# Batches 0 and 1 of an attention and MLP kernel: heads transposed straight from their load by column tiles, and one Ln, Exp and normalise for two units

## The chip, the cores and the metric

The kernel runs on one core of one Trainium2 chip. A core has TensorE (PE in the profile; matmuls and transposes, results in the PSUM banks), VectorE (DVE), ScalarE (ACT), GpSimd (POOL; here it only issues transfers) and SyncE (SP; likewise). The metric is the time on the device for one execution, in microseconds: the median of several runs. Before the change it is 430.69 us (three runs, 430.52 to 430.87).

## What is computed

Attention over 8 batches, 12 heads, 448 positions and 64 features a head, with one added to the denominator of the softmax; then a two-layer MLP with a squared ReLU on the 3584 tokens.

```python
def _attn_ref(q, k, v):
    scale = 1.0 / np.sqrt(q.shape[-1])
    scores = scale * np.matmul(q, k.transpose(0, 1, 3, 2))
    m = np.max(scores, axis=-1, keepdims=True)
    e = np.exp(scores - m)
    attn = e / (np.sum(e, axis=-1, keepdims=True) + np.exp(-m) + 1e-09)
    return np.matmul(attn, v).astype(np.float32)

def _moe_ref(x, w_in, w_out):          # x: 3584 x 768, from all heads; d_ff = 2048
    h = x @ w_in
    r = np.maximum(h, 0.0)
    g = r * r
    return (g @ w_out).astype(np.float32)
```

## The kernel before

The instructions of each engine stand in the order in which the program names them; a pool's buffer is given out again when its last reader is done. Work goes by units: a unit is a pair of heads and a stretch of queries. Batch 0 is cut in two stretches of 192 and 256 queries, so that units 0 to 5 are its pairs with 192 queries, units 6 to 11 the same pairs with 256; units 12 to 17 are batch 1, with all 448 queries, and so on. `RUN` is 4 and `P` is 112: a head's 448 positions lie as 112 partitions of 4 each. `NPAIR` is 6, `D` 64, `S` 448.

Batches 2 to 7 are transposed by the DMA. Batches 0 and 1 come in their natural order, are regrouped on VectorE so that the two heads of a pair lie side by side, and are transposed on TensorE, 128 columns (two heads) at a time:

```python
    def regroup(b, pr):
        for name in "qk":
            f = flat.tile([P, RUN, 2, D], FP16, name=f"flat{name}")
            nc.vector.tensor_copy(f, naturals[name, b, pr].rearrange("p h t d -> p t h d"))
            flats[name, b, pr] = f

    def transposes(b, pr):
        tp = m_psum.tile([128, 2, 512], FP16, name="mp")
        for i, name in enumerate("qk"):
            for s in range(RUN):
                nc.tensor.transpose(tp[:, i, P * s:P * s + P], flats[name, b, pr][:, s], ident[0:P, 0:P])
        if b not in qks:
            qks[b] = qk_pool.tile([128, 3, COLS], FP16, name="qk")
        nc.vector.tensor_copy(qks[b][:, 0:2, pr * S:(pr + 1) * S], tp[:, :, 0:S])
```

The scores of a unit are matmuls into one of two score buffers (`s_psum`, two banks each), and ScalarE's exponential (L155) empties them into `et`. VectorE adds the four chunks of `et` into `es` (L200 to L208). Then:

```python
    def values(u, et, xp, c):
        b, pr, _, n = u
        for kk in (2 * c, 2 * c + 1):
            for h in range(2):
                nc.tensor.matmul(xp[64 * h:64 * h + 64, 0:n], vns[b][:, 2 * pr + h, kk, :],
                                 of_head(chunk(et, u, c, kk), u, h), start=(kk == 0), stop=(kk == RUN - 1))

    def row_sums(u, es):
        n = u[3]
        total = es[:, 0:2 * S] if n == S else es[:, 4 * S - 2 * n:4 * S].rearrange("p (h n) -> p h n", h=2)
        zp = m_psum.tile([128, 512], FP32, name="mp")
        for h in range(2):
            nc.tensor.matmul(zp[64 * h:64 * h + 64, 0:n], ones, of_head(total, u, h), start=True, stop=True)
        rcp = z_pool.tile([128, S], FP32, name="rcp")
        nc.scalar.activation(out=rcp[:, 0:n], in_=zp[:, 0:n], func=AF.Ln, bias=one_b)
        nc.scalar.activation(out=rcp[:, 0:n], in_=rcp[:, 0:n], func=AF.Exp, scale=-1.0)
        return rcp

    def normalise(u, xp, rcp):
        b, pr, q0, n = u
        if b // 2 not in xts:
            xts[b // 2] = xt_pool.tile([128, DCH, 2 * S], FP16, name="xt")
        c = b % 2 * S + q0
        nc.vector.tensor_mul(xts[b // 2][:, pr, c:c + n], xp[:, 0:n], rcp[:, 0:n])
```

The MLP runs between the pieces of the units, a share at a time, so that TensorE has other work while it waits. For its first block (128 tokens) a ReLU in two of four groups goes to ScalarE:

```python
            else:
                nc.vector.tensor_scalar(out=rt[:, 0:m], in0=hp[:, 0:m], scalar1=0.0, scalar2=None, op0=ALU.max)
            g = g_pool.tile([128, 512], FP16, name=f"g{f0}")
            nc.vector.tensor_mul(g[:, 0:m], rt[:, 0:m], rt[:, 0:m])
```

The loop over units, and the warming matmuls ahead of it, which multiply zeros. (b, p) is pair p of batch b; (0, p) is transposed in unit p - 1, (1, p) in unit 8 + p. GpSimd issues the loads in this order: values and q, k of batch 0; half of `w_in`; q, k of (1,0) to (1,2); the rest of `w_in`; q, k of (1,3) to (1,5); half of batch 1's values; `w_out`:

```python
# ... (tables of when each pair is regrouped and transposed, keep_warm, take_up)
    keep_warm(3)
    regroup(0, 1)
    et = es = None
    share = [0.0]

    def take_up(i):
# ...
    for i in range(NU + 1):
        u = units[i] if i < NU else None
        prev = units[i - 1] if i > 0 else None
        xp = rcp = None
        if prev:
            pet, pes = et, es
            xp = x_psum.tile([128, 512], FP32, name="xp")
        if u:
            b, pr = u[0:2]
            if pr == 0 and 0 < b and b + 1 < B:
                load_v(b + 1, 0, NPAIR)
                stage(b + 1)
            et = e_pool.tile([P, RUN * 2 * S], FP16, name="et")
            es = e_pool.tile([P, 4 * S], FP16, name="es")
            scores(u, et, 0)
            if i == 0:
                keep_warm(4)
            elif i < NPAIR:
                keep_warm(1)
                scores(u, et, 1)
            if i == NPAIR:
                rcp = row_sums(prev, pes)
                values(prev, pet, xp, 0)
                values(prev, pet, xp, 1)
                normalise(prev, xp, rcp)
                take_up(i - 1)
            if i in transpose_at:
                transposes(*transpose_at[i])
            if i in regroup_at and i < NPAIR:
                regroup(*regroup_at[i])
            drain(share[0] * (0.45 if i != NPAIR else 0.0))
            if i == 0 or i >= NPAIR:
                scores(u, et, 1)
        if prev and i != NPAIR:
            rcp = row_sums(prev, pes)
            values(prev, pet, xp, 0)
            values(prev, pet, xp, 1)
            if i < NPAIR:
                keep_warm(1)
        if i in regroup_at and i >= NPAIR:
            regroup(*regroup_at[i])
        halved[0] = u is not None
        drain(share[0] * 0.15)
        for step in range(3):
            if u:
                add_chunks(u, et, es, step)
            drain(share[0] * (0.15, 0.1, 0.15)[step])
        halved[0] = False
        if prev and i != NPAIR:
            normalise(prev, xp, rcp)
            take_up(i - 1)
        if u and b and pr == 2 and b + 1 < B:
            transposed_loads(b + 1)
    drain(1e12)


# ---- launch: one core; inputs and outputs as the reference has them ----
_INS = ['q', 'k', 'v', 'moe_w_in', 'moe_w_out']
_OUTS = [((3584, 768), 'float32')]


def kernel(**inputs):
    import numpy as _np
    import concourse.bacc as _bacc
    import concourse.tile as _tile
    from concourse import mybir as _mybir
    from concourse.bass_utils import run_bass_kernel_spmd as _run

    nc = _bacc.Bacc("TRN2", target_bir_lowering=False, num_devices=1)
    arrays, args = {}, []
    for name in _INS:
        a = _np.ascontiguousarray(inputs[name])
        if a.dtype.kind in "iu":
```

`queue` takes up MLP parts once their tokens are done: after unit 5 the first layer for tokens 0 to 127, after unit 11 the first layer for tokens 128 to 383 and the second for 0 to 383. `drain(x)` puts in MLP matmuls worth about x ns; with `halved` set, each is issued as two of 64 columns.

Of the kernel before, what the change touches and what calls it, by code (L numbers as in the profile page):

```python
# [15 lines left out]
def kernel(  # L16
# [9 lines left out]
    nc = tc.nc  # L26
# [21 lines left out]
    flat = ctx.enter_context(tc.tile_pool(name="flat", bufs=3))  # L48
    qk_pool = ctx.enter_context(tc.tile_pool(name="qk", bufs=2))
    e_pool = ctx.enter_context(tc.tile_pool(name="e", bufs=2))  # L50
    z_pool = ctx.enter_context(tc.tile_pool(name="z", bufs=1))
    g_pool = ctx.enter_context(tc.tile_pool(name="g", bufs=2))
    r_pool = ctx.enter_context(tc.tile_pool(name="r", bufs=3))
# [18 lines left out]
    whole, vns, qks, xts, naturals, flats, stages = {}, {}, {}, {}, {}, {}, {}  # L72
# [64 lines left out]
    def regroup(b, pr):  # L137
        for name in "qk":
            f = flat.tile([P, RUN, 2, D], FP16, name=f"flat{name}")
            nc.vector.tensor_copy(f, naturals[name, b, pr].rearrange("p h t d -> p t h d"))  # L140
            flats[name, b, pr] = f

    def transposes(b, pr):
        tp = m_psum.tile([128, 2, 512], FP16, name="mp")
        for i, name in enumerate("qk"):
            for s in range(RUN):
                nc.tensor.transpose(tp[:, i, P * s:P * s + P], flats[name, b, pr][:, s], ident[0:P, 0:P])  # L147
# [47 lines left out]
    def add_chunks(u, et, es, step):  # L195
        n = u[3]
        if n == S:
            e, f = et.rearrange("p (k x) -> p k x", k=RUN), es.rearrange("p (k x) -> p k x", k=2)
            if step < 2:
                nc.vector.tensor_add(f[:, step], e[:, 2 * step], e[:, 2 * step + 1])  # L200
            else:
                nc.vector.tensor_add(f[:, 0], f[:, 0], f[:, 1])  # L202
        elif step == 1:
            nc.vector.tensor_add(es[:, 0:4 * n], et[:, 0:4 * n], et[:, 4 * n:8 * n])  # L204
        elif step == 2:
            f = es[:, 0:4 * n].rearrange("p (h j n) -> p h j n", h=2, j=2)
            o = es[:, 4 * S - 2 * n:4 * S].rearrange("p (h n) -> p h n", h=2)
            nc.vector.tensor_add(o, f[:, :, 0, :], f[:, :, 1, :])  # L208
# [10 lines left out]
    def values(u, et, xp, c):  # L219
        b, pr, _, n = u  # L220
        for kk in (2 * c, 2 * c + 1):
            for h in range(2):
                nc.tensor.matmul(xp[64 * h:64 * h + 64, 0:n], vns[b][:, 2 * pr + h, kk, :],  # L223
                                 of_head(chunk(et, u, c, kk), u, h), start=(kk == 0), stop=(kk == RUN - 1))

    def row_sums(u, es):
        n = u[3]
# [248 lines left out]
```

The softmax here doesn't subtract the row's maximum and nothing guards it: scores larger than these inputs give would overflow.

## Time and profile before

| what | value |
| --- | --- |
| time, median of 3 | 430.69 us |
| span of the profiled execution | 430.7 us |
| busy: TensorE, VectorE, ScalarE, GpSimd | 421.4, 246.6, 247.6, 33.2 us |
| exponentials of the scores (L155) | 192, 165.9 us busy |
| Ln and Exp for the denominators (L233, L234) | 54 and 54, 32.2 and 28.9 us busy |
| normalise (L242) | 54, 30.6 us busy |
| regroup in the first 50 us (L140) | 24 copies and casts, 8.6 us busy |
| transposes on TensorE (L147) | 96, half of q and half of k |
| moved by DMA | 47.56 MB, 110 GB/s over the span |
| first scores of unit 0, of unit 6, of unit 12 | at 6.26, 23.56 and 42.58 us |

One execution is recorded by the hardware profiler. A line of a group or of the timeline names the line of the kernel, the engine, the operation, and what is written and read (buffer numbers left out), with sizes as partitions x elements; then how many, and how long. In brackets stands how long the engine was idle before the instruction and what ended that wait. Matmuls are pipelined, so the busy time of one is longer than the distance between the starts of two; the distance is what counts for the pace. The granted clock is the share of TensorE's full clock. A DMA share over 1 means that packets overlapped on the 16 DMA engines.

### The profile page before, as it was taken

The page shows a single profiled execution, that of the slowest core. Times are in us where ns is not written, and L with a number is a line of the kernel's source. Part 1 is how long each engine was busy: PE and PEld are TensorE (multiplying, and loading weights), DVE is VectorE, ACT ScalarE, POOL GpSimd, SP SyncE. Part 2 cuts the span into 40 slices and gives each one's busy share as a digit, 9 for nine tenths or more (in the row PEclk, how much of TensorE's full clock was granted, in tenths as well). Part 3 has the DMA queues.
Part 4 walks back from the last instruction along what each step waited for, and adds up shares of the span by engine and source line. Part 5 has one row for each costly group of instructions (what it writes and reads, how often), then busy time and mean ns, then how long its engine had stood idle before and what let it go on. Part 6 is the DMA issues. An engine that isn't in the chain of part 4 may idle for free.

```text
span 430.7 us, 9136 instructions
## 1 busy us (share of the span) xinstructions
PE 421.4 (98%) x3975; PEld 248.1 (58%) x3975; DVE 246.6 (57%) x489; ACT 247.6 (57%) x359; POOL 33.2 (8%) x52
## 2 busy tenths in 40 slices
PE   8989899999999999999999999999999999999996
PEld 3557675554465666554556665654556666564454
DVE  4759695268822596348842488248762278428700
ACT  4698867764555756674456755774555655740011
POOL 7541100010000100010000100030000000000000
PEclk9699899999999999999999999999999999999999
DMA  9999999399312893259811697139902200010022
GB/s 200 197 197 204 209 218 180 96 156 210 58 39 75 146 215 63 74 83 214 128 37 52 99 223 127 39 61 207 192 3 75 74 3 2 37 54 22 0 75 74
DMA packets 79129, 47.56 MB, mean 110 GB/s; under 512 B 50672, under 2 KB 75120, under 8 KB 78704
## 3 DMA queue, kind: packets, MB, share of 16 engines
q0 software_dynamic: 24160, 22.17, 32.2%
q1 hardware_dynamic: 54208, 24.11, 25.5%
q10 hardware_dynamic: 720, 0.69, 0.6%
q8 instruction: 31, 0.51, 0.5%
q14 instruction: 10, 0.08, 0.1%
HBM read 45.71 MB, written 19.32 MB: 151 GB/s over the span
## 4 chain that ended last, share of the span: by engine, by line
PE 92%; DVE 2%; ACT 2%; DMA 2%; issue 1%; ACTq 0%
PE mp L254 37%; PE mp L252 31%; PE sp L187 9%; PE xp L223 8%; PE mp L231 3%; PE sp L175 2%; DMA kr<-in_k_dram 2%; ACT et L155 1%; PE mp L147 1%; PE mp L376 1%; DVE es L204 1%; DVE qk L150 0%; ACT rcp L233 0%; DVE xt L242 0%; DVE es L208 0%
## 5 line engine op out<-in xcount | busy, mean ns | idle before, releaser
L155 ACT ACTIVATE et<-sp 112x896 f16<-112x896 f32 (+2 forms) x192 | 165.9, 914 | 109.8 <-PE sp L187 92.1
L200 DVE TENSOR_TENSOR es<-et 112x896 f16<-112x896 f16 x84 | 51.6, 622 | 103.5 <-ACT et L155 103.4
L274 DVE TENSOR_SCALAR rt<-mp 128x512 f16<-128x512 f32 (+1 forms) x122 | 77.4, 635 | 35.3 <-PE mp L252 24.1
L254 PE MATMUL mp<-xt,win 128*128 128x512 f16 (+3 forms) x456 | 84.8, 339 | 0.0
L254 PE MATMUL mp<-wout,g 128*128 128x512 f16 (+1 forms) x471 | 82.3, 330 | 0.0
L252 PE MATMUL mp<-wout,g 128*64 128x256 f16 (+1 forms) x850 | 71.9, 322 | 0.0
L252 PE MATMUL mp<-xt,win 128*64 128x384 f16 (+3 forms) x816 | 71.2, 325 | 0.2 <-DVE xt L242 0.2
L254 PEld LDWEIGHTS <-g 128*128 128x128 f16 x471 | 44.3, 98 | 33.9 <-issue 2.5
L304 ACT ACTIVATE ot<-mp 128x512 f32<-128x512 f32 (+1 forms) x56 | 27.3, 487 | 63.4 <-PE mp L254 51.7
L254 PEld LDWEIGHTS <-win 128*128 128x128 f16 x456 | 41.6, 98 | 36.6 <-issue 2.1
L252 PEld LDWEIGHTS <-g 128*64 128x64 f16 x850 | 47.7, 110 | 19.4
L252 PEld LDWEIGHTS <-win 128*64 128x64 f16 x816 | 45.4, 110 | 22.6 <-issue 1.0
L276 DVE TENSOR_TENSOR g<-rt 128x512 f16<-128x512 f16 (+1 forms) x124 | 49.5, 399 | 6.5 <-ACT rt L272 2.3
L223 PE MATMUL xp<-et,vn 112*64 112x448 f16 (+2 forms) x432 | 46.5, 338 | 0.3 <-DVE xt L242 0.3
L187 PE MATMUL sp<-qk 64*112 64x224 f16 x576 | 42.8, 268 | 0.0
L187 PEld LDWEIGHTS <-qk 64*112 64x112 f16 x576 | 26.9, 128 | 25.4 <-issue 25.4
L233 ACT ACTIVATE rcp<-mp,one_b 128x448 f32<-128x448 f32 (+2 forms) x54 | 32.2, 597 | 3.1 <-PE mp L231 2.8
L242 DVE TENSOR_TENSOR xt<-xp,rcp 128x448 f16<-128x448 f32 (+2 forms) x54 | 30.6, 566 | 3.5 <-ACT rcp L234 3.5
L223 PEld LDWEIGHTS <-vn 112*64 112x64 f16 x432 | 24.8, 112 | 10.3 <-issue 0.6
L234 ACT ACTIVATE rcp<-rcp 128x448 f32<-128x448 f32 (+2 forms) x54 | 28.9, 535 | 1.7
L78 POOL DMA_DIRECT2D vn<-in_v_dram x10 | 9.0, 902 | 243.2 <-PE xp L223 229.1
L202 DVE TENSOR_TENSOR es<-es 112x896 f16<-112x896 f16 x42 | 26.1, 623 | 1.0
(36 smaller groups left out, 136.5 us busy)
## 6 DMA issues: line engine op xcount, KB each, us to landing
out_dram<-ot SPq DMA_DIRECT2D x11, 384.0 KB, 2.3
vn<-in_v_dram POOLq DMA_DIRECT2D x6, 672.0 KB, 9.1
stage_q<-in_q_dram POOLq DMA_DIRECT2D x5, 676.0 KB, 11.1
stage_k<-in_k_dram POOLq DMA_DIRECT2D x5, 676.0 KB, 14.0
win<-in_moe_w_in_dram POOLq DMA_DIRECT2D x8, 384.0 KB, 13.8
wout<-in_moe_w_out_dram POOLq DMA_DIRECT2D x4, 768.0 KB, 20.2
out_dram<-ot SPq DMA_DIRECT2D x8, 288.0 KB, 2.6
out_dram<-ot SPq DMA_DIRECT2D x8, 192.0 KB, 2.7
```

The source lines that it names most:

```text
L155: nc.scalar.activation(out=out_, in_=in_, func=AF.Exp, scale=scale)
L187: nc.tensor.matmul(sp[:, odd, h * (S // 2):(h + 1) * (S // 2)], qk[r, which, kx:kx + 2 * P - 1:2], qk[r, 0, x:x + S // 2], start=True, sto ...
L200: nc.vector.tensor_add(f[:, step], e[:, 2 * step], e[:, 2 * step + 1])
L223: nc.tensor.matmul(xp[64 * h:64 * h + 64, 0:n], vns[b][:, 2 * pr + h, kk, :], of_head(chunk(et, u, c, kk), u, h), start=(kk == 0), stop=(k ...
L233: nc.scalar.activation(out=rcp[:, 0:n], in_=zp[:, 0:n], func=AF.Ln, bias=one_b)
L234: nc.scalar.activation(out=rcp[:, 0:n], in_=rcp[:, 0:n], func=AF.Exp, scale=-1.0)
L242: nc.vector.tensor_mul(xts[b // 2][:, pr, c:c + n], xp[:, 0:n], rcp[:, 0:n])
L252: nc.tensor.matmul(out_[x:x + 64], lhsT[:, x:x + 64], rhs, start=start, stop=stop)
L254: nc.tensor.matmul(out_, lhsT, rhs, start=start, stop=stop)
L274: nc.vector.tensor_scalar(out=rt[:, 0:m], in0=hp[:, 0:m], scalar1=0.0, scalar2=None, op0=ALU.max)
L276: nc.vector.tensor_mul(g[:, 0:m], rt[:, 0:m], rt[:, 0:m])
L304: nc.scalar.activation(out=ot[:, n0:n1], in_=op[:, 0:n1 - n0], func=AF.Copy, scale=OUT_SCALE)
```

## The change

It does two things, for the units of batch 0 and the transposes of batches 0 and 1.

First, it drops the regroup. Each head is transposed by itself from the tile that it was loaded into, as a column tile: head 0 of a pair goes to partitions 0 to 63 of the result, head 1 to 64 to 127. There are 16 transposes of 64 columns a pair instead of 8 of 128. Only the three pairs that are loaded in float32 are still cast on VectorE, in the order in which they lie.

Second, two units of batch 0 share one accumulator bank for the values, one row-sums bank, one Ln, one Exp and one normalise (six of each for the twelve units). The loop over the first twelve units is written apart. In it the values of the unit before no longer stand behind its row sums: the row sums of two units come together, behind the values of the second. To have the sums of two units at hand, `es` gets a pool of its own with three buffers, half the size, and the first half sums go to a buffer `half`. The first MLP block has one ReLU on ScalarE instead of two. `flat` and `r` go from three to two buffers. Batches 1 to 7 keep their unit by unit form.

```diff
@@ -45,12 +45,13 @@
     xt_pool = ctx.enter_context(tc.tile_pool(name="xt", bufs=2))
     nat = ctx.enter_context(tc.tile_pool(name="nat", bufs=1))
     v_pool = ctx.enter_context(tc.tile_pool(name="v", bufs=2))
-    flat = ctx.enter_context(tc.tile_pool(name="flat", bufs=3))
+    flat = ctx.enter_context(tc.tile_pool(name="flat", bufs=2))
     qk_pool = ctx.enter_context(tc.tile_pool(name="qk", bufs=2))
     e_pool = ctx.enter_context(tc.tile_pool(name="e", bufs=2))
+    es_pool = ctx.enter_context(tc.tile_pool(name="es", bufs=3))
     z_pool = ctx.enter_context(tc.tile_pool(name="z", bufs=1))
     g_pool = ctx.enter_context(tc.tile_pool(name="g", bufs=2))
-    r_pool = ctx.enter_context(tc.tile_pool(name="r", bufs=3))
+    r_pool = ctx.enter_context(tc.tile_pool(name="r", bufs=2))
     osb_pool = ctx.enter_context(tc.tile_pool(name="osb", bufs=2))
 
     s_psum = ctx.enter_context(tc.tile_pool(name="s_psum", bufs=2, space=bass.MemoryType.PSUM))
@@ -134,17 +135,19 @@
             )
 
 
-    def regroup(b, pr):
+    def cast(b, pr):
         for name in "qk":
-            f = flat.tile([P, RUN, 2, D], FP16, name=f"flat{name}")
-            nc.vector.tensor_copy(f, naturals[name, b, pr].rearrange("p h t d -> p t h d"))
-            flats[name, b, pr] = f
+            f = flat.tile([P, 2, RUN, D], FP16, name=f"flat{name}")
+            nc.vector.tensor_copy(f, naturals[name, b, pr])
+            naturals[name, b, pr] = f
 
     def transposes(b, pr):
         tp = m_psum.tile([128, 2, 512], FP16, name="mp")
         for i, name in enumerate("qk"):
             for s in range(RUN):
-                nc.tensor.transpose(tp[:, i, P * s:P * s + P], flats[name, b, pr][:, s], ident[0:P, 0:P])
+                for h in range(2):
+                    nc.tensor.transpose(tp[64 * h:64 * h + 64, i, P * s:P * s + P],
+                                        naturals[name, b, pr][:, h, s, :], ident[0:P, 0:P])
         if b not in qks:
             qks[b] = qk_pool.tile([128, 3, COLS], FP16, name="qk")
         nc.vector.tensor_copy(qks[b][:, 0:2, pr * S:(pr + 1) * S], tp[:, :, 0:S])
@@ -192,20 +195,19 @@
         if n < S:
             exp(et[:, 0:RUN * 2 * n].rearrange("p (c h x) -> p c h x", c=2, h=2)[:, c], two[:, :, 0:2 * n])
 
-    def add_chunks(u, et, es, step):
+    def add_chunks(u, et, es, half, step):
         n = u[3]
         if n == S:
-            e, f = et.rearrange("p (k x) -> p k x", k=RUN), es.rearrange("p (k x) -> p k x", k=2)
+            e = et.rearrange("p (k x) -> p k x", k=RUN)
             if step < 2:
-                nc.vector.tensor_add(f[:, step], e[:, 2 * step], e[:, 2 * step + 1])
+                nc.vector.tensor_add((es, half[:, 0:2 * S])[step], e[:, 2 * step], e[:, 2 * step + 1])
             else:
-                nc.vector.tensor_add(f[:, 0], f[:, 0], f[:, 1])
+                nc.vector.tensor_add(es, es, half[:, 0:2 * S])
         elif step == 1:
-            nc.vector.tensor_add(es[:, 0:4 * n], et[:, 0:4 * n], et[:, 4 * n:8 * n])
+            nc.vector.tensor_add(half[:, 0:4 * n], et[:, 0:4 * n], et[:, 4 * n:8 * n])
         elif step == 2:
-            f = es[:, 0:4 * n].rearrange("p (h j n) -> p h j n", h=2, j=2)
-            o = es[:, 4 * S - 2 * n:4 * S].rearrange("p (h n) -> p h n", h=2)
-            nc.vector.tensor_add(o, f[:, :, 0, :], f[:, :, 1, :])
+            f = half[:, 0:4 * n].rearrange("p (h j n) -> p h j n", h=2, j=2)
+            nc.vector.tensor_add(es[:, 0:2 * n].rearrange("p (h n) -> p h n", h=2), f[:, :, 0, :], f[:, :, 1, :])
 
     def of_head(e, u, h):
 
@@ -216,30 +218,40 @@
             return e.rearrange("p (h x) -> p h x", h=2)[:, h]
         return e.rearrange("p (o h x) -> p h o x", o=2, h=2)[:, h]
 
-    def values(u, et, xp, c):
+    def values(u, et, xp, o=0):
         b, pr, _, n = u
-        for kk in (2 * c, 2 * c + 1):
+        for kk in range(RUN):
             for h in range(2):
-                nc.tensor.matmul(xp[64 * h:64 * h + 64, 0:n], vns[b][:, 2 * pr + h, kk, :],
-                                 of_head(chunk(et, u, c, kk), u, h), start=(kk == 0), stop=(kk == RUN - 1))
-
-    def row_sums(u, es):
-        n = u[3]
-        total = es[:, 0:2 * S] if n == S else es[:, 4 * S - 2 * n:4 * S].rearrange("p (h n) -> p h n", h=2)
+                nc.tensor.matmul(xp[64 * h:64 * h + 64, o:o + n], vns[b][:, 2 * pr + h, kk, :],
+                                 of_head(chunk(et, u, kk // 2, kk), u, h), start=(kk == 0), stop=(kk == RUN - 1))
+
+    def row_sums(us, sums):
+
+        n = us[0][3]
+        m = n * len(us)
         zp = m_psum.tile([128, 512], FP32, name="mp")
-        for h in range(2):
-            nc.tensor.matmul(zp[64 * h:64 * h + 64, 0:n], ones, of_head(total, u, h), start=True, stop=True)
-        rcp = z_pool.tile([128, S], FP32, name="rcp")
-        nc.scalar.activation(out=rcp[:, 0:n], in_=zp[:, 0:n], func=AF.Ln, bias=one_b)
-        nc.scalar.activation(out=rcp[:, 0:n], in_=rcp[:, 0:n], func=AF.Exp, scale=-1.0)
+        for j, (u, es) in enumerate(zip(us, sums)):
+            total = es[:, 0:2 * n]
+            if n < S:
+                total = total.rearrange("p (h n) -> p h n", h=2)
+            for h in range(2):
+                nc.tensor.matmul(zp[64 * h:64 * h + 64, j * n:(j + 1) * n], ones, of_head(total, u, h),
+                                 start=True, stop=True)
+        rcp = z_pool.tile([128, 512], FP32, name="rcp")
+        nc.scalar.activation(out=rcp[:, 0:m], in_=zp[:, 0:m], func=AF.Ln, bias=one_b)
+        nc.scalar.activation(out=rcp[:, 0:m], in_=rcp[:, 0:m], func=AF.Exp, scale=-1.0)
         return rcp
 
-    def normalise(u, xp, rcp):
-        b, pr, q0, n = u
+    def normalise(us, xp, rcp):
+        b, pr, q0, n = us[0]
         if b // 2 not in xts:
             xts[b // 2] = xt_pool.tile([128, DCH, 2 * S], FP16, name="xt")
         c = b % 2 * S + q0
-        nc.vector.tensor_mul(xts[b // 2][:, pr, c:c + n], xp[:, 0:n], rcp[:, 0:n])
+        if len(us) == 1:
+            nc.vector.tensor_mul(xts[b // 2][:, pr, c:c + n], xp[:, 0:n], rcp[:, 0:n])
+        else:
+            two = [t[:, 0:2 * n].rearrange("p (j n) -> p j n", j=2) for t in (xp, rcp)]
+            nc.vector.tensor_mul(xts[b // 2][:, pr:pr + 2, c:c + n], *two)
 
 
     gts = {}
@@ -268,7 +280,7 @@
                         yield n / 2.4
             m = per * n
             rt = r_pool.tile([128, 512], FP16, name="rt")
-            if t0 == 0 and f0 % 8 == 0:
+            if t0 == 0 and f0 == 8:
                 nc.scalar.activation(out=rt[:, 0:m], in_=hp[:, 0:m], func=AF.Relu)
             else:
                 nc.vector.tensor_scalar(out=rt[:, 0:m], in0=hp[:, 0:m], scalar1=0.0, scalar2=None, op0=ALU.max)
@@ -364,24 +376,14 @@
         ready[(b + 2) * NPAIR - 1] = [(1, t0, n), (2, t0, n)]
         t0 += n
 
... (tables and the lines ahead of the loop; transposes stand where they stood)
     def take_up(i):
         if i in ready:
@@ -389,62 +391,101 @@
                 queue(*part)
             share[0] = left[0] / NPAIR
 
-    for i in range(NU + 1):
+    share = [0.0]
+    ets, ess = {}, {}
+    xp = None
+
+    keep_warm(9)
+    cast(0, 0)
+    transposes(0, 0)
+    keep_warm(3)
+    cast(0, 1)
+
+    def end_two(i, xp):
+
+        two = units[i - 2:i]
+        rcp = row_sums(two, (ess.pop(i - 2), ess.pop(i - 1)))
+        normalise(two, xp, rcp)
+        take_up(i - 1)
+
+
+    for i in range(2 * NPAIR):
+        u = units[i]
+        et = ets[i] = e_pool.tile([P, RUN * 2 * S], FP16, name="et")
+        es = ess[i] = es_pool.tile([P, 2 * S], FP16, name="es")
+        half = e_pool.tile([P, 1024], FP16, name="half")
+        if i % 2:
+            xp = x_psum.tile([128, 512], FP32, name="xp")
+        scores(u, et, 0)
+        if i == 0:
+            keep_warm(4)
+        elif i < NPAIR:
+            keep_warm(1)
+            scores(u, et, 1)
+        if i == NPAIR:
+            values(units[i - 1], ets.pop(i - 1), xp, units[i - 1][3])
+            end_two(i, xp)
+        if i in transpose_at:
+            transposes(*transpose_at[i])
+        if i == 0:
+            cast(0, 2)
+        if i > NPAIR:
+            drain(share[0] * 0.45)
+        if i == 0 or i >= NPAIR:
+            scores(u, et, 1)
+        if i and i != NPAIR:
+            values(units[i - 1], ets.pop(i - 1), xp, (i - 1) % 2 * units[i - 1][3])
+        if i < NPAIR:
+            keep_warm(1)
+        halved[0] = True
+        drain(share[0] * 0.3)
+        add_chunks(u, et, es, half, 1)
+        if i and i % 2 == 0 and i != NPAIR:
+            end_two(i, xp)
+        add_chunks(u, et, es, half, 2)
+        drain(share[0] * 0.25)
+        halved[0] = False
+
+
     for i in range(2 * NPAIR, NU + 1):
... (as the old loop for its units from 12 on; the first of them also ends the last pair:)
+        if first:
+            done = units[i - 2:i]
+            values(prev, ets.pop(i - 1), xp, prev[3])
+            rcp = row_sums(done, (ess.pop(i - 2), ess.pop(i - 1)))
+        else:
+            done = [prev]
+            rcp = row_sums(done, (ess.pop(i - 1),))
+            values(prev, ets.pop(i - 1), xp)
... (shares of the MLP and sums as before)
+        normalise(done, xp, rcp)
+        take_up(i - 1)
```

## The prediction

> **What bounds the kernel now.** I read the page's first part, then the table by windows, then the timeline of the first 60 us, then the issues with their times to landing.
>
> ```profile
> PE 421.4 (98%) x3975; PEld 248.1 (58%) x3975; DVE 246.6 (57%) x489; ACT 247.6 (57%) x359; POOL 33.2 (8%) x52
> ...
> PEclk9699899999999999999999999999999999999999
> ```
>
> TensorE is busy 98% of the span, so at first sight nothing can be won on other engines. But a busy share is an average. The digit row of the granted clock has a 6 and an 8 in its second and fifth slices (10.8 us each), and the windows show why:
>
> ```profile
> 9.00:12.00 3.00, 2.16 (x28) 1.29 (x24) 2.08 (x6) 2.07 (x5) 2.09 (x3) 0.93 1.45 196
> 12.00:15.00 3.00, 3.00 (x21) 1.48 (x21) 1.58 (x5) 1.98 (x3) 1.90 (x3) 0.50 1.45 197
> ...
> 30.00:33.00 3.00, 1.97 (x33) 1.45 (x31) 2.36 (x6) 2.85 (x5) 0.74 (x1) 1.00 1.46 196
> ...
> 39.00:42.00 3.00, 3.00 (x60) 2.45 (x61) 2.83 (x8) 2.69 (x6) 0.00 (x0) 1.00 1.17 210
> 42.00:45.00 3.00, 2.21 (x26) 1.39 (x23) 2.63 (x7) 2.97 (x5) 0.00 (x0) 1.00 1.16 211
> 45.00:48.00 3.00, 2.59 (x19) 1.16 (x17) 2.61 (x7) 2.97 (x6) 0.09 (x1) 0.62 1.17 212
> ...
> 51.00:54.00 3.00, 3.00 (x45) 2.28 (x46) 1.22 (x3) 2.57 (x4) 0.00 (x0) 1.00 1.19 208
> ```
>
> The columns are the window, its length, busy time of PE, PEld, DVE, ACT and POOL, then granted clock, DMA share and GB/s. From 51 us on TensorE has no gap and full clock: nothing there can be shortened except its own work. Before that it has gaps (2.16, 1.97, 2.21 of 3 us) and two stretches at half clock. The DMA column says something else: over 1.4 and 197 GB/s from 9 to 39 us[...]. The timeline says what the gaps wait for:
>
> ```profile
> 32.15 0.30 PE L231 MATMUL mp<-es,ones 112*64 112x256 f16 x2 [1.00 <-DVE es L208]
> ...
> 32.88 0.28 DVE L140 COPY flatq<-qn 112x512 f16<-112x512 f16 x1
> 33.08 0.29 DVE L140 COPY flatk<-kn 112x512 f16<-112x512 f16 x1
> ...
> 40.56 0.37 PE L147 MATMUL mp<-ident,flatq 112*128 112x112 f16 x4
> ...
> 48.27 0.42 DVE L242 TENSOR_TENSOR xt<-xp,rcp 128x256 f16<-128x256 f32 x1
> ...
> 48.69 2.35 PE L254 MATMUL mp<-xt,win 128*128 128x256 f16 x18
> ```
>
> The row sums (L231) stand before the values in PE's order and wait 1.00 us for VectorE, which is nearly full from 33 to 45 us with sums, regroups, evictions and normalises. The saturated stretch begins with the MLP matmuls at 48.69. The 430.7 us span is thus 48.7 us of start plus 382 us that the change hardly touches. Only the start can move, by at most how much earlier that MLP may begin.
>
> [...] 22 half-width MLP matmuls of 128 columns go from 28.71 to 29.42 us, 32 ns each, eight full ones from 30.18 to 30.73 us, 69 ns each. [...] The trace has the two stretches at half rate begin near 11.7 and 45.8 us[...]. [...] Ln takes 420 ns at 192 and 478 at 256 columns, Exp 363 and 417.
>
> **The change part by part.**
> *ScalarE.* Twelve Ln and twelve Exp of 192 or 256 columns become six and six of 384 or 512. With the slopes above (0.88 ns a column): Ln of 384 is 420 + 0.88 x 192 = 589 ns against 2 x 420, Exp of 384 is 363 + 0.84 x 192 = 525 against 2 x 363; together 0.45 us saved per pair of units, and as much at 512. Six pairs: 2.7 us. One Relu (584 ns) moves to VectorE. Per unit of the first six, ScalarE falls from 2.28 us (et starts at 19.86 and 22.14) to about 2.0.
> *VectorE.* The regroup stays as a cast for three pairs and goes for nine: 18 copies, 0.20 us from start to start (32.88, 33.08), 3.6 us. The normalises save about 0.16 us a pair (352 ns at 192, 418 at 256: 1.03 ns a column, so 681 at 512 against 836), 0.9 us in all; the moved Relu costs 0.69. Net 3.8 us, in units 6 to 11 from 3.1-3.4 us a unit to about 2.5.
> *TensorE.* Each pair takes 16 transposes of 64 rows out instead of 8 of 128. At 32 ns that is 0.51 us against 0.40 (29.78 to 30.18), +0.11 us; 1.3 us over twelve pairs, most of it within gaps. MLP work is the same. The row sums now follow the values, so the waits on L208 (1.00 at 32.15, 0.71 at 24.69, 0.48 at 11.23) leave the path. In exchange the values of the first unit of a pair wait for the normalise of the pair before, in one accumulator buffer; I estimate up to 0.5 us per pair there.
> *Start of units.* Unit 2's scores come at 12.44; without the row sums' wait about 11.7. PE work of a unit in batch 0 is then 0.3 + 0.32 + 0.3 (scores, warming, scores) + 0.51 + 0.45 (values) + 0.32 + half of 0.22 = 2.3 us, more than ScalarE's 2.0. Unit 6, at 23.56 now, comes near 21 if the clock stays full and near 23 if the half-clock stretch from 11.7 remains. Units 6 to 10 at about 3.0 us, plus 0.3 for the later double normalise, put unit 11's transposes of (1,3) at 36.5 to 39 us instead of 40.56.
>
> *And there the transfers catch it.* The timeline has the issue of k of batch 1, pairs 3 to 5, and the answer for this tile, cut to that issue, has its time to landing:
>
> ```profile
> 23.72 0.77 POOL L92 DMA_DIRECT2D kn<-in_k_dram  x1 [1.20 <-DMA win<-in_moe_w_in_dram]
> ```
>
> ```profile
> DMA to landing us min/median/max: 15.4/15.4/15.4
> ```
>
> So it lands at 39.1 us. The regroup of (1,3) on VectorE came at 39.40, right behind it. Nothing in the change makes the queue shorter: the same bytes in the same order at 197 GB/s. Transposes of (1,3) can't start before about 39.2, so this point gains 1.4 us and no more, however fast the units before it are.
>
> *From there to the MLP.* Now 40.56 to 48.69, 8.1 us, of which 1.1 us is PE waiting on ScalarE (0.72 and 0.41 before the scores of unit 12) and some 1.4 us half clock. After, call the start T = 39.2. ScalarE has caught up while PE waited, but then has two exponentials of about 1.0 us (unit 11; one of them already done), four of 0.83 (unit 12), Ln and Exp of 512 (1.3) and the normalise (0.7, behind three sums) in a row: T + 1.5 + 1.0 + 3.3 + 1.3 + 0.9 = T + 8.0. The MLP needs pairs 4 and 5 from that one normalise, but can do the first four of six products before, about 0.5 us. Its effective start is T + 7.6 = 46.8, 1.9 us earlier. [...] The half-clock end of the old stretch (to 49.2) goes too, worth some 0.25 us. The extra 0.11 us of transposes of (1,5) is within these. I take 1.5 us: **429.2 us**.
>
> **Rivals.** *A: VectorE and ScalarE were the bound of the start, so the full saving of 3 to 4 us is paid out (427).* For it: VectorE almost without gap from 33 to 45. Against it: the landing at 39.1, only 0.3 us before the old kernel used it. It would be right if PE could run on past that load, but its order is fixed. *B: the load's wait is paid twice, through the clock.* [...] the long chain of the double normalise puts another gap before the MLP[...]. That would make 430 to 432. For it: the trace shows both stretches after gaps only a little over 1 us. Against it: the old kernel pays two such stretches already, and one may go. *C: transposes as column tiles do not overlap* (64-wide weight loads take 110 ns in the trace, 128-wide ones 98): [...] 430 to 431. Against it: the 32 ns above, of the same half-width form. *D: a later load.* Batch 2's transposed loads end at about 78 us and are used at 82.44, 4.7 us of slack; a gain of 2 us does not reach it.
>
> **Range and chances.** The load caps the gain near 3 us even if everything after it goes well; the clock and the chain of the double normalise could take it all and up to half a microsecond more. 427.4 to 431.2 should hold it 8 times in 10. Two per cent is 8.6 us, far beyond the cap[...]: faster 0.02, within 0.97, slower 0.01.
>
> **What would show it.** Right: 18 copies fewer on VectorE and six activations each of Ln and Exp wider; L149's transposes 16 in about 0.5 us; a PE wait on the load of kn just before the transposes of (1,3), which start at 39 to 39.5; the first 256-column MLP matmuls at 46.5 to 48; the steady part unchanged, 382 us long within 0.5. Wrong: those transposes start well before 39 (the load moved), or well after (units did not speed up); transposes at 1 us a pair; a third stretch of half clock, or none; steady units longer because of two instead of three eviction buffers.

## The result, and the profile after

The changed kernel takes 430.21 us (median of 4, 430.07 to 430.31) against 430.72 us for the kernel before beside it: ratio 0.9988, 95% interval 0.9971 to 1.0006. In a second measurement it was 430.27 against 430.55 us, ratio 0.9994 (0.9984 to 1.0005). The gain is 0.3 to 0.5 us, and neither interval excludes none at all.

The spans of the two profiles say something else: 430.7 us before, 428.2 after. First the page of the changed kernel, its engine line and the digits of the granted clock:

```profile
PE 419.0 (98%) x4070; PEld 246.7 (58%) x4070; DVE 242.3 (57%) x466; ACT 244.9 (57%) x346; POOL 33.4 (8%) x52
...
PEclk9999999999999999999999999999999999999999
```

VectorE has 23 records fewer (18 copies and 6 normalises less, one Relu more), ScalarE 13 fewer (six Ln, six Exp, one Relu), as the diff says. The 6 and the 8 of the clock are gone. Then TensorE's timeline up to the stretch in which it never stops. Columns: start, length, line, operation, and in brackets the idle time and what ended it.

```profile
16.36 0.52 PE L225 MATMUL xp<-et,vn 112*64 112x192 f16 x8 [0.38 <-DVE xt L254]
...
21.43 0.52 PE L225 MATMUL xp<-et,vn 112*64 112x192 f16 x8 [0.89 <-DVE xt L254]
...
25.39 0.47 PE L264 MATMUL mp<-xt,win 128*64 128x128 f16 x10 [1.12 <-DVE xt L254]
...
37.70 0.39 PE L149 MATMUL mp<-ident,qn 112*64 112x112 f16 x8
38.75 0.39 PE L149 MATMUL mp<-ident,kn 112*64 112x112 f16 x8 [0.65 <-DMA kn<-in_k_dram]
...
40.44 0.67 PE L264 MATMUL mp<-xt,win 128*64 128x128 f16 x18
...
43.25 0.40 PE L178 MATMUL sp<-qk 64*112 64x448 f16 x2 [0.41 <-ACT et L158]
...
45.71 0.61 PE L266 MATMUL mp<-xt,win 128*128 128x256 f16 x4
46.83 1.69 PE L266 MATMUL mp<-xt,win 128*128 128x256 f16 x14 [0.51 <-DVE xt L254]
48.45 0.58 PE L178 MATMUL sp<-qk 64*112 64x448 f16 x4
```

The row sums' waits on L208 are gone. In their place stand waits on the shared normalise (L254): 0.38 and 0.89 us for the values of units 2 and 4, 1.12 and 0.51 for the MLP. And TensorE now waits for k of (1,3) to arrive, at 38.75 us. The 256-column MLP begins at 45.71 instead of 48.69.

So the profiles differ by 2.5 us, and the medians by 0.5 at most. The experiments are about where the other 2 us are.

### The profile page after: what moved, and what is told of

Same layout as the page of the kernel before. It is cut to its first block, busy times and chain, and to the rows that moved or that the text cites. A ratio compares the mean times of both kernels' runs of the same rounds, so it can differ in the third digit from the quotient of the medians.

```text
span 428.2 us, 9293 instructions
## 1 busy us (share of the span) xinstructions
PE 419.0 (98%) x4070; PEld 246.7 (58%) x4070; DVE 242.3 (57%) x466; ACT 244.9 (57%) x346; POOL 33.4 (8%) x52
## 3 DMA queue, kind: packets, MB, share of 16 engines
HBM read 45.71 MB, written 19.32 MB: 152 GB/s over the span
## 4 chain that ended last, share of the span: by engine, by line
PE 92%; DMA 3%; ACT 2%; DVE 2%; issue 0%; DVEq 0%; ACTq 0%
PE mp L266 38%; PE mp L264 31%; PE sp L190 9%; PE xp L225 8%; DMA kn<-in_k_dram 3%; PE mp L238 3%; PE mp L386 2%; PE sp L178 2%; PE mp L149 1%; ACT et L158 1%; DVE qk L153 0%; ACT rcp L241 0%; DVE xt L254 0%; DVE half L207 0%; ACT rcp L242 0%
## 5 line engine op out<-in xcount | busy, mean ns | idle before, releaser
L203 DVE TENSOR_TENSOR half<-et 112x896 f16<-112x896 f16 x42 | 26.1, 622 | 54.5 <-ACT et L158 54.4
L203 DVE TENSOR_TENSOR es<-et 112x896 f16<-112x896 f16 x42 | 26.1, 621 | 49.1 <-ACT et L158 49.1
L225 PE MATMUL xp<-et,vn 112*64 112x448 f16 (+2 forms) x432 | 45.7, 332 | 1.4 <-DVE xt L254 1.4
L241 ACT ACTIVATE rcp<-mp,one_b 128x448 f32<-128x448 f32 (+2 forms) x48 | 30.7, 640 | 2.7 <-PE mp L238 2.7
L225 PEld LDWEIGHTS <-vn 112*64 112x64 f16 x432 | 23.7, 110 | 12.3 <-issue 2.6
L242 ACT ACTIVATE rcp<-rcp 128x448 f32<-128x448 f32 (+2 forms) x48 | 27.7, 577 | 1.5
L251 DVE TENSOR_TENSOR xt<-xp,rcp 128x448 f16<-128x448 f32 x42 | 25.9, 617 | 2.4 <-ACT rcp L242 2.4
```

The costliest lines, as they stand in the source:

```text
L203: nc.vector.tensor_add((es, half[:, 0:2 * S])[step], e[:, 2 * step], e[:, 2 * step + 1])
L225: nc.tensor.matmul(xp[64 * h:64 * h + 64, o:o + n], vns[b][:, 2 * pr + h, kk, :], of_head(chunk(et, u, kk // 2, kk), u, h), start=(kk == 0 ...
L241: nc.scalar.activation(out=rcp[:, 0:m], in_=zp[:, 0:m], func=AF.Ln, bias=one_b)
L242: nc.scalar.activation(out=rcp[:, 0:m], in_=rcp[:, 0:m], func=AF.Exp, scale=-1.0)
```

## Experiments

Theory: the load of k for (1,3) to (1,5) sets when unit 11's transposes start, for any kernel that reaches unit 11 early; what the units before gain is lost in waiting for it. Rivals: VectorE's pace was the bound (then either half of the change should pay by itself); the half-clock stretches make the difference of the profiles. The kernel before was measured beside every run.

**before_again**: the kernel before with no edit, for a second profile.

> The kernel before, unchanged, for its own profile and the clock of each execution. Clock theory: the profiled execution of before (432.5 us for a median of 430.7) was one with more half-clock time than most, so the profile made the change look 2.5 us better while the times say 0.5 us. Then the executions here show a mean clock above 0.988 and spans near 428.9 us, and a new profile has less than the two half-clock stretches of the first (or later ones). Rival: both stretches are in every execution of before, every clock is near 0.988 and the span near 430.7; then the profile's difference is real and the times hide it elsewhere. The ratio to itself is 1.000 either way.

430.43 us, ratio to itself 0.9996 (0.9985 to 1.0008). Its profile has a span of 428.7 us and a clock of 0.999; the first one of before had 430.7 and 0.988. The first had been taken of an execution of 432.5 us, 1.8 us above the median. Its span of 430.7 looks like the median of 430.69, but a time is some 1.8 us longer than its span (430.45 and 428.7 here, 430.07 and 428.2 in the change). In the page of before_again the clock digits are all nines:

```profile
PEclk9999999999999999999999999999999999999999
```

And its timelines of VectorE and TensorE show the load as a wait in the kernel before too:

```profile
39.11 0.29 DVE L140 COPY flatk<-kn 112x512 f16<-112x512 f16 x1 [1.76 <-DMA kn<-in_k_dram]
```

```profile
39.46 0.37 PE L147 MATMUL mp<-ident,flatk 112*128 112x112 f16 x4 [1.16 <-DVE flatk L140]
...
41.28 0.25 PE L252 MATMUL mp<-xt,win 128*64 128x128 f16 x2
...
46.52 0.71 PE L254 MATMUL mp<-xt,win 128*128 128x256 f16 x5
47.44 1.58 PE L254 MATMUL mp<-xt,win 128*128 128x256 f16 x13 [0.21 <-DVE xt L242]
48.95 0.59 PE L175 MATMUL sp<-qk 64*112 64x448 f16 x4
```

With full clock the kernel before was already early enough to wait for k. The change brings the transposes of k from 39.46 to 38.75. Half of these 0.71 us is the VectorE copy that stood between the landing and the transposes (39.11 to 39.46, of which the copy itself is 0.29). The other half is that k landed earlier: issued at 24.3 us in both profiles, it took 14.4 us instead of 14.8. Why is not shown. From there to the scores that follow the first 18 MLP matmuls it takes 9.70 us (38.75 to 48.45) instead of 9.49 (39.46 to 48.95): TensorE waits less, but is busy for 8.57 us instead of 7.92, with 16 more of the half-width MLP matmuls ahead of unit 12 (18 at 40.44, where the kernel before has 2). 0.71 less 0.21 is 0.50, the difference of the spans, 428.7 to 428.2; the other 2.0 us, 430.7 to 428.7, lie between two executions of the same kernel.

**transposes_only**: the kernel before, with the column-tile transposes alone.

```diff
-    regroup_at = {pr - 2: (0, pr) for pr in range(2, NPAIR)}
+    regroup_at = {0: (0, 2)}
-        regroup_at[NPAIR + 1 + pr] = (1, pr)
```
(and `regroup` and `transposes` as in the change)

> The kernel before with the first half of the change alone: column-tile transposes from the load, no regroup for nine pairs; units still end one by one, row sums ahead of the values. Load theory (the transposes of (1,3) wait for their load until 38.7 to 39.1 us, whatever the units before them do): 430.0 to 430.6 us, within 0.15% of before, since VectorE's 3.6 us of copies were hidden behind that load. Rival (VectorE was the bound of units 6 to 11): 1.5 to 2.5 us faster, 428.3 to 429.2.

430.01 against 430.67 us, ratio 0.9985 (0.9973 to 0.9997): within the load theory's 430.0 to 430.6, and not the rival's 1.5 to 2.5 us faster. Half of the change gives as much as the whole. The load is waited for longer than in the change:

```profile
38.99 0.39 PE L148 MATMUL mp<-ident,kn 112*64 112x112 f16 x8 [0.94 <-DMA kn<-in_k_dram]
```

**pairs_only**: the changed kernel with the regroup and 128-column transposes put back for all pairs.

```diff
-            f = flat.tile([P, 2, RUN, D], FP16, name=f"flat{name}")
-            nc.vector.tensor_copy(f, naturals[name, b, pr])
+            f = flat.tile([P, RUN, 2, D], FP16, name=f"flat{name}")
+            nc.vector.tensor_copy(f, naturals[name, b, pr].rearrange("p h t d -> p t h d"))
```
(issued at the places of the kernel before; 8 transposes of 128 columns a pair)

> The changed kernel with the second half alone: regroup and 128-column transposes as before for all twelve pairs, but two units share accumulator, row sums, Ln, Exp and normalise. Load theory: 430.0 to 431.0 us; VectorE has its 18 copies back, and the waits of the values on the shared normalise stay, so unit 11 comes at 38 to 40 us, close behind the load. Rival (the pairs are what pays): 429.5 or less.

430.99 against 430.67 us, ratio 1.0004 (0.9996 to 1.0013). The pairs by themselves pay nothing; the fastest of 13 executions took 430.86 us, and 22 of the 38 of before were faster than that. The starts of the scores, in us, and the transposes of k of (1,3), read from the five timelines, show what they do:

| | unit 2 | unit 6 | unit 2 to 6 | k of (1,3) | unit 12 |
| --- | --- | --- | --- | --- | --- |
| before_again | 11.73 | 20.64 | 8.91 | 39.46 | 41.46 |
| transposes_only | 12.39 | 20.98 | 8.59 | 38.99 | 40.95 |
| pairs_only | 11.74 | 22.07 | 10.33 | 39.45 | 42.04 |
| after | 12.09 | 22.20 | 10.11 | 38.75 | 41.03 |
| late_transposes (below) | | | | in unit 12 | 39.85 |

With the shared normalise units 2 to 5 take 1.4 to 1.5 us longer, the opposite of its purpose. Up to the transposes of k nobody notices, since all of them wait for the same load. Behind it pairs_only loses 0.58 us more against before_again (unit 12 at 42.04 and 41.46): its values wait 0.36 us for the shared normalise at 40.98, and it has the 16 more MLP matmuls there too.

**late_transposes**: the changed kernel, with the transposes of batch 1 one unit later.

```diff
-        transpose_at[NPAIR + 2 + pr] = (1, pr)
+        transpose_at[NPAIR + 3 + pr] = (1, pr)
```

> The changed kernel with the transposes of batch 1 one unit later, (1,p) in unit 9+p, so that (1,3) falls in unit 12, well after its load. Load theory: the wait of 0.65 us on the load of k goes, unit 12 begins 0.5 to 0.7 us earlier than 41.03, and the time falls by 0.3 to 0.7 us against the changed kernel, to 429.5 to 429.9; more only if nothing else takes its place (ScalarE's queue in unit 12). Rival (the wait on the load is idle time that the row of ScalarE work behind it would have cost anyway): within 0.1 us of 430.2.

429.40 against 430.67 us, ratio 0.9969 (0.9957 to 0.9982). The wait for k is gone, 0.47 us of wait for the shared normalise has come in its place, and unit 12 begins at 39.85 instead of 41.03:

```profile
38.79 0.63 PE L225 MATMUL xp<-et,vn 112*64 112x256 f16 x8 [0.47 <-DVE xt L254]
...
39.85 0.59 PE L178 MATMUL sp<-qk 64*112 64x448 f16 x4
40.36 0.39 PE L149 MATMUL mp<-ident,qn 112*64 112x112 f16 x8
```

(In this execution unit 6 began 0.36 us earlier than in the first profile of the change, at 21.84. That is not what the gain comes from: in after_again, below, it began at 21.92, and unit 12 came at 41.15.) Of the 1.18 us at unit 12, 0.5 goes back, as the transposes of (1,5) now lie in the saturated stretch (51.87 to 52.39); the span is 427.5 against 428.2. The forecast (429.5 to 429.9) was a little too cautious.

**after_again**: the changed kernel once more.

> The changed kernel, unchanged, in as many rounds as the others, so that its gain of 0.5 us (interval up to no difference) can be told apart from none, and its half-clock stretches counted against those of before. Expected: 0.9985 to 0.9992 of before. Clock theory: fewer executions near 431.5 us than the 13 of 38 that before had, because the shared row sums leave fewer gaps ahead of unit 3. Rival: the stretches come as often[...].

0.9994, given above: just outside the forecast. Two of its 13 executions took over 431 us (mean granted clock 0.996 and 0.995); of before's, 14 of 46 in the same measurement. The direction is the clock theory's, the numbers are small.

**transposes_only_late**: the kernel before with the column-tile transposes alone, and those of batch 1 one unit later.

```diff
-    regroup_at = {pr - 2: (0, pr) for pr in range(2, NPAIR)}
+    regroup_at = {0: (0, 2)}
-        regroup_at[NPAIR + 1 + pr] = (1, pr)
-        transpose_at[NPAIR + 2 + pr] = (1, pr)
+        transpose_at[NPAIR + 3 + pr] = (1, pr)
```
(and `regroup` and `transposes` as in the change)

> The first half of the change alone (column-tile transposes, no regroup, units ending one by one) with the transposes of batch 1 one unit later. transposes_only waited 0.94 us for the load of k. Load theory: most of that is paid out, 429.2 to 429.5 us against its 430.0, at least as good as the pairs with late transposes (429.4). Rival (the pairs pay once the load is out of the way): 429.8 or more, clearly behind 429.4.

430.01 against 430.55 us, ratio 0.9987 (0.9976 to 0.9997): by its median no faster than transposes_only (430.01), and 0.6 us behind late_transposes. The load theory's figure failed, and the rival's, that the pairs pay once the load is out of the way, came true. The wait for k is gone here as well, but the profile, of an execution of 430.16 us, has a longer wait for VectorE's sums in unit 8, and then a stretch at about half speed: the eight matmuls of the values take 0.80 us at 28.98 (up to 29.78) and 0.44 at 33.59 (up to 34.03). The mean granted clock of this execution was 0.996.

```profile
28.64 0.30 PE L233 MATMUL mp<-es,ones 112*64 112x256 f16 x2 [1.40 <-DVE es L210]
28.98 1.07 PE L225 MATMUL xp<-et,vn 112*64 112x256 f16 x8
29.78 1.43 PE L254 MATMUL mp<-xt,win 128*64 128x128 f16 x22
...
33.59 0.60 PE L225 MATMUL xp<-et,vn 112*64 112x256 f16 x8
34.03 0.78 PE L254 MATMUL mp<-xt,win 128*64 128x128 f16 x22
...
38.56 0.36 PE L148 MATMUL mp<-ident,kn 112*64 112x112 f16 x8
```

In transposes_only the same wait was 0.88 us, behind the transposes that have now moved away. The 14 executions lie between 428.82 and 431.15 us. The fastest is 0.8 us below the fastest of transposes_only (429.67) and 0.3 below that of late_transposes (429.12), and the four fastest, 428.82 to 429.36 us, had a mean granted clock of 0.999 or 1.000, the other ten 0.996. So the wait for the load seems to be paid out in those four. That is argued from times and clocks: none of the four was profiled.

**after_slowed** and **late_slowed**: eight score matmuls added ahead of unit 11, once where the load is waited for and once where it isn't.

```diff
+    twice = units[8:10]
-                for h in range(2):
+                for h in (0, 1, 0, 1) if u in twice and c == 0 else (0, 1):
```

> The changed kernel with the first score matmuls of units 8 and 9 issued twice into the same place: 8 more matmuls of 256 columns, 0.09 us each from start to start, 0.7 us more TensorE work ahead of the transposes of (1,3). Load theory: it fills the wait on k (0.65 us), so within 0.15 us of the changed kernel. Rival (TensorE's or VectorE's pace in units 6 to 11 is the bound): 0.5 to 0.7 us slower.

> The same 8 extra matmuls in the kernel with late transposes, where no load is waited for. Load theory: now they cost their full time, 0.5 to 0.7 us on 429.4. Rival: about nothing, as ScalarE's queue in units 11 and 12 would be the bound.

after_slowed: 430.26 us, the changed kernel beside it 430.27. No cost is seen, as the load theory says. But the added work is smaller than the forecasts have it:

```profile
27.40 0.64 PE L178 MATMUL sp<-qk 64*112 64x256 f16 x8
27.98 0.39 PE L149 MATMUL mp<-ident,qn 112*64 112x112 f16 x8
...
38.44 0.39 PE L149 MATMUL mp<-ident,kn 112*64 112x112 f16 x8 [0.84 <-DMA kn<-in_k_dram]
```

Eight score matmuls take 0.58 us up to the transposes; four take 0.36 in the changed kernel (28.11 to 28.47). The two units together have 0.44 us more, not 0.7, and half of that fills the wait for the shared normalise in unit 9 (0.17 us in the changed kernel, none here). From the start of unit 6 to the transposes of q of (1,3) it is 15.72 us (21.49 to 37.21), against 15.50 in after_again (21.92 to 37.42). So under the rival this run had to be 0.2 us slower, not 0.5 to 0.7, and 0.2 is little beside the scatter of the executions (all but one between 429.75 and 430.49). The run agrees with the load theory and does not decide. What the profile shows directly is that TensorE still waits for k, 0.84 us.

late_slowed: 429.62 us, ratio 0.9977 (0.9970 to 0.9984), about 0.2 us more than late_transposes (429.40 and 429.44), where 0.5 to 0.7 was forecast. That forecast was wrong for the same two reasons: from the start of unit 6 to the scores behind the 18 MLP matmuls it is 25.64 us (22.15 to 47.79), against 25.43 in late_again (21.86 to 47.29).

**late_again**: late_transposes once more.

> The kernel with late transposes once more, with more rounds and beside the three below: 429.2 to 429.6 us, 0.997 of before, no different from its first measurement.

429.44 us, ratio 0.9973 (0.9962 to 0.9984). It repeats: both times the interval lies wholly below 1. The kernel is faster than both kernels of this case, by 1.2 us than before; against the changed kernel it is 0.8 us by medians of different measurements, 0.7 to 0.8 by spans (427.5 twice, against 428.2 and 428.3).

**late_split**: late transposes, and units 4 and 5 end singly.

```diff
-        two = units[i - 2:i]
+        two = units[i - 1:i] if i in (5, 6) else units[i - 2:i]
-        if i % 2:
+        if i % 2 or i == 6:
             xp = x_psum.tile([128, 512], FP32, name="xp")
-        if i and i % 2 == 0 and i != NPAIR:
+        if i and (i % 2 == 0 or i == 5) and i != NPAIR:
             end_two(i, xp)
```

> Late transposes, and units 4 and 5 end one by one (own accumulator, row sums, Ln, Exp and normalise each), the other pairs as in the change. In the changed kernel the MLP's first group waited 1.12 us for the shared normalise of 4 and 5, and late_slowed showed that waits on shared normalises can hide extra TensorE work. Theory (latency of the shared normalise is the next bound): Ln, Exp and normalise of one unit are 0.16 + 0.16 + 0.2 us shorter, the MLP starts 0.3 to 0.5 us earlier, and 0.1 to 0.4 us of it is paid out: 429.0 to 429.3. Rival (one more Ln and Exp on ScalarE, 0.8 us, delays the exponentials by as much): 429.4 or more.

430.95 us, ratio 1.0005 (0.9992 to 1.0018): 1.5 us slower than late_again beside it. The shorter latency only moved the wait: the values of unit 5 now wait for the normalise of unit 4 in the single accumulator, directly after unit 4's values have waited for the normalise of units 2 and 3.

```profile
21.39 0.52 PE L225 MATMUL xp<-et,vn 112*64 112x192 f16 x8 [0.90 <-DVE xt L254]
...
23.73 0.85 PE L225 MATMUL xp<-et,vn 112*64 112x192 f16 x8 [0.94 <-DVE xt L251]
...
25.28 1.41 PE L264 MATMUL mp<-xt,win 128*64 128x128 f16 x18
26.61 0.68 PE L178 MATMUL sp<-qk 64*112 64x256 f16 x4
```

(L225 at 21.39 is the values of unit 4, at 23.73 of unit 5.) From there to about 30.5 us the matmuls take half as long again or more: four score matmuls 0.61 us from start to start at 24.67 and 28.18, against 0.36 at 30.64. The table by windows has the granted clock in the third column from the right:

```profile
21.00:24.00 3.00, 1.67 (x19) 1.06 (x20) 1.78 (x5) 2.64 (x5) 0.77 (x1) 0.94 1.45 196
24.00:27.00 3.00, 2.98 (x36) 1.92 (x32) 0.82 (x2) 1.90 (x4) 1.54 (x2) 0.50 1.45 198
27.00:30.00 3.00, 3.00 (x32) 2.13 (x30) 0.70 (x3) 2.05 (x2) 1.41 (x2) 0.50 1.45 196
```

TensorE was busy 1.67 of 3 us, and for the following 6 us its granted clock was 0.50. The profiled execution took 432.15 us, at a mean granted clock of 0.991. The forecast gain shows nowhere: the fastest of the 14 took 429.52 us, above late_again's median. The rival's figure, 429.4 or more, came true, but what the profile shows is the new wait and the clock; that the added Ln and Exp delay the exponentials is not shown.

**early_load**: the changed kernel with q and k of (1,3) to (1,5) ahead of the last quarter of `w_in`.

```diff
-    for i in range(4, 8):
+    for i in range(4, 6):
         load_win(i, 8)
     load_natural(1, 3, 6)
+    for i in range(6, 8):
+        load_win(i, 8)
```

> The changed kernel with the loads of q and k for (1,3) to (1,5) issued ahead of the last quarter of w_in instead of behind it. Load theory, strict form (what counts is the bytes in the queue up to unit 11): k lands near 35 us and its wait of 0.65 to 1.05 us goes, but the last eighth of w_in now lands near 39 us and the MLP matmuls of unit 11 wait for it; net gain 0 to 0.5 us, 429.7 to 430.2. Rival (only that one tile was late): 429.4 to 429.6, as much as with late transposes.

429.77 against 430.60 us, ratio 0.9983 (0.9975 to 0.9991), within the strict form's range. The wait moved to the weights, one unit earlier, and is shorter:

```profile
36.87 0.25 PE L264 MATMUL mp<-xt,win 128*64 128x128 f16 x2 [0.37 <-DMA win<-in_moe_w_in_dram]
...
38.06 0.36 PE L149 MATMUL mp<-ident,kn 112*64 112x112 f16 x8
```

The second wait that was forecast, in unit 11, didn't come. This run changes only the order of loads, and its time is 0.4 to 0.5 us below the changed kernel's (430.21 and 430.27, in other measurements): when the tiles arrive from the queue is what bounds the start up to here.

**before_filled**: the kernel before, with three warming matmuls in unit 12's gap.

```diff
+            if i == 2 * NPAIR:
+                keep_warm(3)
             if i == 0 or i >= NPAIR:
                 scores(u, et, 1)
```

> The kernel before with three warming matmuls (0.64 us) in unit 12, where TensorE waited 0.72 us for ScalarE ahead of the second half of the scores. Clock theory (the executions near 431.5 us, 27 of 84 so far, are those in which the gaps of units 11 to 13 cost a half-clock stretch): they become rare, 0 to 2 of 14, and the median falls to 430.2 to 430.4. Rival (they come from something else, such as the transfers): still a third of the executions, median 430.5 to 430.7.

430.63 us, ratio 1.0002 (0.9994 to 1.0010), and 4 of 14 executions over 431 us, beside 7 of 36 of the kernel before. The forecast failed: filling that gap does not make the long executions rare. The rival's median came true, but what else the long executions come from is not shown. The gap at the load of k (1.53 us in this profile) was left as it was. Whether it, or another, is the one that counts was not tried.

## Why the prediction was right or wrong

**The bound and the load: right.** It said that the transposes of (1,3) would start at 39 to 39.5, with a wait on k just before. Those of k start at 38.75, with 0.65 us of wait; k landed 0.4 us earlier than the 39.1 that was worked out. late_transposes and early_load confirm the bound in two ways: moving the use behind the landing pays, moving the load ahead pays. after_slowed agrees, but is too small to decide. Rival A (VectorE's full 3.6 us paid out) fell with transposes_only.

**The size: 1.5 us forecast, 0.3 to 0.5 measured. The step that failed is the base, "Now 40.56 to 48.69".** That point of departure came from one profile, of an execution 1.8 us above the median, and the gain worked out from it was taken off the median. Two terms of the sum were in that execution and not in the usual one: the transposes of (1,3) at 40.56 (in before_again those of q start at 37.92, and those of k wait until 39.46), and "some 1.4 us half clock" behind them. So the load had held up the kernel before as well, and "this point gains 1.4 us" is 0.7. The chain behind it was right: the wait for the normalise was to end at T + 8.0, and it ended at 46.83, 8.08 us after T = 38.75. The first 256-column MLP matmuls came at 45.71, ahead of the forecast 46.5 to 48; in before_again they come at 46.52. That the measured 430.21 lay in the range of 427.4 to 431.2 was luck: the range took in no gain at all because the clock and the normalise might take the gain back, and not because the base might be too high. The step from the 1.9 us of the chain to 1.5 was the author's estimate.

**The first six units: wrong.** Unit 6 was to come near 21 us at full clock, earlier than before; it comes at 22.20, and before_again has 20.64. 0.4 us of that is there at unit 2 already (12.09, where 11.7 was forecast). For the rest the step is "up to 0.5 us per pair" for the wait on the shared normalise: 0.38 and 0.89 us at the values, and 1.12 at the MLP. The row of row sums, Ln (0.58), Exp (0.52) and normalise (0.56) takes from 14.18 to 16.36 for units 0 and 1, and the TensorE work that was to cover it fills only 1.80 of these 2.18 us. The error cost nothing, because the load hid it.

**Units 6 to 10 at 3.0 us: right** (22.20 to 37.31, 3.02 a unit). **From the load to the MLP** the order was right too: the MLP does four matmuls, then waits 0.51 us for the normalise that starts at 46.09.

**Transposes as column tiles:** forecast 0.51 us for 16. They take 0.41 (13.02 to 13.43) where the values follow and 0.51 (28.47 to 28.98) where full-width MLP matmuls follow, so rival C, with 1 us a pair, is out. Where the 0.10 us between the two comes from is not shown.

**Rival B** (the load's wait paid a second time through the clock) did not happen: after waits of 0.65 us in the first profile of the change and 1.05 us in after_again the mean granted clock of both executions was 1.000. late_split and transposes_only_late slowed down behind other waits (0.90 and 0.94 us, mean clock 0.991; 1.40 us, 0.996). The steady part is as forecast: from 48.45 to the end 379.8 us, from 48.95 in before_again also 379.8.

## What to carry to other kernels

Before sizing a gain, compare the time of the profiled execution, not its span, with the median: here the difference, 1.8 us, was larger than the gain in question, and it lay in just the stretch that the change was about. Where loads come at one steady rate (here 194 to 201 GB/s in every 3 us from 9 to 39 us, before and after), work out when each tile can arrive from the queue; a faster chain ahead of that only waits longer. On top of the change, moving the use behind the arrival (one line, some 0.8 us) was worth more than the change itself; without the pairs the same line moved nothing in the median, as another wait grew. Merging small operations of two units saves time (Ln and Exp of 384 columns take 0.58 and 0.52 us here, of 192 columns 0.42 and 0.36 each time) but puts the longer row behind the later unit; with a single accumulator, that came back as waits of 0.38 and 0.89 us.

## What was not expected of the hardware

Executions of one kernel differ in the granted clock. The profiles show none, one or two stretches at half clock (0.50 in windows that lie within one), between 11 and 50 us after the start. Worked out from the granted clocks by windows of 3 us they are 3.4 or 6.8 us long: in late_split 0.94, 0.50, 0.50 and 0.92 over four windows make 0.36 + 3 + 3 + 0.48 = 6.8 us of half clock, in the first profile of the kernel before 0.62 and 0.81 from 45 to 51 us make 2.28 + 1.14 = 3.4. Within one kernel they go with the time of the execution: the kernel before has none at 430.45 us (mean clock 0.999) and two at 432.5 (0.988).

What decides on a stretch is not settled. That waits of TensorE bring it, as the clock theory has it, was the author's estimate from the first profile of the kernel before. In the 4 us ahead of each stretch TensorE waited 1.1 to 1.8 us: 0.42, 0.36 and 0.48, then 0.72 and 0.41, in that profile; 0.71 and 0.41 in transposes_only; 1.40 in transposes_only_late; 0.90 and 0.94 in late_split. But the kernel before waits the same 0.72 and 0.41 us in unit 12 in both its profiles, and only one of them has half clock there; and 1.53 us in before_filled were followed by none (mean clock 1.000).
